# TensorE's order by an estimate of VectorE's backlog, and keys copied by ScalarE, in a fused attention and gated-MLP kernel

## The chip, the core and the metric

The kernel runs on one NeuronCore of a Trainium2 chip. Its engines are TensorE (PE in the profile, with its weight loads as PEld), VectorE (DVE), ScalarE (ACT), GpSimd (POOL) and SyncE (SP), which here only issues DMAs. Each engine executes its own instructions strictly in the order in which the program lists them; they wait for each other by semaphores. The metric is the device time of one execution in microseconds; the time of a kernel is the median of several runs.

## The reference

A sequence of 2048 tokens with 640 features is normalised per token. Branch A is attention with 32 heads of 20 features over 4 segments of 512 tokens, with a memory carried from segment to segment; branch B is a gated MLP with 1536 hidden features. All tensors are bf16.

```python
xn = _layernorm(x, axis=-1)
q, k, v = xn @ wq, xn @ wk, xn @ wv          # 32 heads x 20, 4 segments x 512
for s in range(4):
    p = softmax(qs @ ks.T * Dh**-0.5 + causal_mask)
    a_dot = p @ vs
    a_mem = (phi(qs) @ M) / (phi(qs) @ z + 1e-6)
    o = g * a_mem + (1.0 - g) * a_dot         # g = sigmoid(beta), per head
    M = M + phi(ks).T @ vs                    # phi(t) = t + 1 if t > 0 else exp(t)
    z = z + sum(phi(ks))
s = o @ wo
h = sigmoid(xn @ w_gate) * (xn @ w_up)
out = x + s * silu(h @ w_down)
```

## The kernel before

Four segments of 512 tokens are pipelined. While segment n has its attention scores computed, the same stretch of program also holds the projections of segment n+1, the MLP of segment n, and the output projection of segment n-1. A segment is cut into 20 slots (`NSLOT`). Each slot has one group of score matmuls (`Sps`, four row tiles side by side), one exponential of 2048 columns on ScalarE (`pt`), a causal select on GpSimd, and the weighing of an earlier group by the values (`Aps`, many matmuls of 21 columns). Between them the program puts matmul units from two sources:

- **tasks**, with a due time in slots. They are in a heap; when the position `pos` (in slots) passes a task's time, it is taken out. A task that is a generator (`k_chunk`, `q_chunk`, `q_bound`, `v_tile`, `o_proj`, `mem_read`, `m_update`) goes into the list `ready`; any other (a DMA, a step of VectorE) is issued at once. `later(lag, ...)` makes a task due `lag * R` slots from now, with R = 20/24.
- **bulk**, the gate, up and down projections of the MLP in their order.

`step` gives the next matmul: of the unit in hand, else of the first one in `ready`, else of bulk. `advance` moves `pos` by each matmul's cost (`T512` = 0.216 us for 512 columns, `T320` = 0.136) over the segment's budget for one slot. So the order on all engines is written out when the program is made; nothing is decided on the chip.

PSUM has 4 banks for the scores, one for `Aps` and three for everything else (the pool `ps_d`, tag "d"): a matmul unit needs one of these three, and it is free again when VectorE or ScalarE has read it. What each unit leaves to these engines:

- `k_chunk`: a copy of `psk` to bf16 (`evacuate`: ScalarE in segment 0, VectorE in the others), then a VectorE maximum of absolute values from the copy (`kabs`, L301). After chunks 2 and 4 the copy goes to DRAM (`stage_out`), and from there to `KT` in another layout (`relay`).
- `q_chunk`: the same copy (`q5`), then absolute values on VectorE (`aq`, L332). `q_bound` multiplies `aq` with `IK` (made from `kabs`) to a bound on each score (`cps`), which goes by `c_out` to DRAM (`Cs`) and by `c_in` into `QT`, where the score matmuls read it.
- `mem_read`: three VectorE instructions (L460 to L463) behind up to three short matmuls (`am`). `m_update`: two per chunk (L442, L443).
- gate: a tanh on ScalarE (`tg`). up: one VectorE instruction (`hT`, L492), which also reads `tg`. down: a tanh on ScalarE (`t`), then VectorE (`aa`, L509). `o_proj`: VectorE L557, and for the second half L563 and the store.
- phi (L400, L401, ScalarE L404, then L408): 5 chunks of k and 5 of q in a segment, at most two at a time.
- `weigh`: L607, L608, L610 on VectorE once per head group.

The startup is written by hand: weight loads and the first four blocks of x on SP's queue, warm-up matmuls, statistics (`ln_stats`), normalising (`ln_norm`, with a TensorE transpose `pT` in segment 0), values of segment 0 (`v_tile`), keys, queries, the staging of both through DRAM, and six units of bulk, before the first scores.

Of the kernel before, what the change touches and what calls it, by code (L numbers as in the profile page):

```python
# [10 lines left out]
P = 128  # L11
S = 2048
D = 640
# [3 lines left out]
NSEG = 4  # L17
# [38 lines left out]
T320 = 0.136  # L56
TPV = 0.0255


@with_exitstack  # L60
def kernel(
# [49 lines left out]
    def run(unit):  # L111
        for _ in unit:
            pass

    def step(keep):
        if cur[0] is None:
            if ready:
                cur[0] = ready.pop(0)
            elif len(bulk) > keep:
                _, fn, a = bulk.pop(0)  # L120
                cur[0] = fn(*a)
            else:
                return None
        cost = next(cur[0], None)
        if cost is None:
            cur[0] = None
            return 0.0
        return cost

    def advance(target, budget, keep):  # L130
        while True:
            while tasks and tasks[0][0] <= pos[0]:
                _, _, _, fn, a = heapq.heappop(tasks)
                if inspect.isgeneratorfunction(fn):
                    ready.append(fn(*a))
                else:
                    fn(*a)
            if pos[0] >= target:
                return
            cost = step(keep)  # L140
            if cost is None:
                pos[0] = min(target, tasks[0][0]) if tasks else target
            else:
                pos[0] += cost / budget
# [4 lines left out]
    def x_load(n, p):  # L149
        t = lnp.tile([P, 2, D], BF, name="xt2")  # L150
        st[n][f"x{p}"] = t
        r0 = n * L + 2 * p * P
        if n == 0:
            for i in range(2):
                nc.sync.dma_start(t[:, i, :], x2[r0 + i * P:r0 + (i + 1) * P, :])
        else:
            nc.sync.dma_start(t[:], x2[r0:r0 + 2 * P, :].rearrange("(i p) d -> p i d", p=P))

# [6 lines left out]

    x_load(0, 0)
    load_proj("v", A_wv, 0, HB)
    x_load(0, 1)
    load_proj("v", A_wv, HB, D)
# [10 lines left out]

    for i in range(2):
        load_glu(i, 0)
        load_glu(i, 1)

# [57 lines left out]
    def ln_stats(n, p, i0=0, i1=2):  # L242
        s = st[n]
        x = s[f"x{p}"]
        if i0 == 0:
            s[f"mv{p}"] = lnp.tile([P, 2, 2], F32, name="mv")
            s[f"rstd{p}"] = lnp.tile([P, 2], F32, name="rstd")
        mv, rstd = s[f"mv{p}"], s[f"rstd{p}"]
        for i in range(i0, i1):
            bs = lnp.tile([P, 2, 6], F32, name="bs")  # L250
            nc.vector.bn_stats(bs[:, 0, :], x[:, i, 0:HB])
            nc.vector.bn_stats(bs[:, 1, :], x[:, i, HB:D])
            nc.vector.bn_aggr(mv[:, i, :], bs[:])
        nc.gpsimd.tensor_scalar(rstd[:, i0:i1], mv[:, i0:i1, 1], EPS, None, op0=ALU.add)
        nc.gpsimd.tensor_tensor(rstd[:, i0:i1], rstd[:, i0:i1], nhalf[:, i0:i1], op=ALU.pow)

    def ln_norm(n, p, i):
        s = st[n]
        if "xnT" not in s:
            s["xnT"] = xpool.tile([P, DC, L], BF, name="xnT")  # L260
        xn = lnp.tile([P, D], BF, name="xn")
        nc.vector.tensor_scalar(xn[:], s[f"x{p}"][:, i, :], s[f"mv{p}"][:, i, 0:1], s[f"rstd{p}"][:, i:i + 1],
# [19 lines left out]

    def evacuate(n, dst, ps):
        if n == 0:
            nc.scalar.copy(dst, ps)
        else:
            nc.vector.tensor_copy(dst, ps)  # L287

    def k_chunk(n, c):
# [5 lines left out]
        for k in range(DC):  # L295
            nc.tensor.matmul(ps[:], lhsT=W["k"][:, k, c * P:(c + 1) * P], rhs=s["xnT"][:, k, :],  # L296
                             start=(k == 0), stop=(k == DC - 1))
            if k < DC - 1:
                yield T512
        evacuate(n, s["k5"][:, c, :], ps[:])  # L300
        nc.vector.tensor_reduce(out=s["kabs"][:, c:c + 1], in_=s["k5"][:, c, :], axis=AX.X, op=ALU.max,  # L301
                                apply_absolute_value=True)
        if c in (2, 4) and n:
            later(0.9, stage_out, n, c // 4, Ks, KT, "k5")
# [6 lines left out]
    def stage_out(n, half, src, dst, name):  # L311
        a, b = ((0, 3), (3, 5))[half]
        st[n][f"out_{name}"] = b
        nc.sync.dma_start(src[n % 2][a * P:b * P, :].rearrange("(c p) n -> p c n", p=P), st[n][name][:, a:b, :])
        if n:
            later(1.0, relay, n, half, src, dst)
            for c in range(a, b):
                later(1.9 if name == "q5" else 0.7, phi_push, n, name, c)

    def q_chunk(n, c):  # L320
# [5 lines left out]
        for k in range(DC):  # L326
            nc.tensor.matmul(ps[:], lhsT=W["q"][:, k, c * P:(c + 1) * P], rhs=s["xnT"][:, k, :],  # L327
                             start=(k == 0), stop=(k == DC - 1))
            if k < DC - 1:
                yield T512  # L330
        evacuate(n, s["q5"][:, c, :], ps[:])
        nc.vector.tensor_scalar(s["aq"][:, c, :].bitcast(U16), s["q5"][:, c, :].bitcast(U16), 0x7FFF, None,  # L332
                                op0=ALU.bitwise_and)
        if c in (2, 4) and n:
            later(0.9, stage_out, n, c // 4, Qs, QT, "q5")
        yield T512

# [58 lines left out]
    def phi(n, src, c):  # L396
# [4 lines left out]
        nc.vector.tensor_scalar(t, t, 1.0, None, op0=ALU.add)  # L401

        def exp():
            nc.scalar.activation(mn[:], mn[:], ACT.Exp)  # L404
            later(0.5, rest)

        def rest():
            nc.vector.tensor_tensor(t, t, mn[:], op=ALU.max)  # L408
            st[n][f"phi_{src}"] = c + 1
# [13 lines left out]
    def m_update(n, cs):  # L423
# [3 lines left out]
        for i, c in enumerate(cs):  # L427
            w = (H1[c] - H0[c]) * VW
            for j in range(4):
                nc.tensor.matmul(dm[:, i, 0:w], lhsT=s["pkt"][:, j, c * P:(c + 1) * P],  # L430
                                 rhs=V[4 * (n % 2) + j][:, H0[c]:H1[c], :].rearrange("p h e -> p (h e)"),
                                 start=(j == 0), stop=(j == 3))
            yield 4 * w / 2400
        for i, c in enumerate(cs):
            w = (H1[c] - H0[c]) * VW
# [9 lines left out]
    def mem_read(n, j, b):  # L445
# [7 lines left out]
        for i, c in enumerate(parts):  # L453
# [3 lines left out]
                             rhs=Mbd[:, c, lo - H0[c]:hi - H0[c], :].rearrange("p h e -> p (h e)"),  # L457
                             start=(i == 0), stop=True, skip_group_check=True)
        rm = opool.tile([P, 16], F32, name="rm", bufs=3)
        nc.vector.scalar_tensor_tensor(out=rm[:], in0=am[:, :, DH], scalar=1e-6,  # L460
# [21 lines left out]
    def up(n, f):  # L482
# [3 lines left out]
        for k in range(DC):  # L486
            nc.tensor.matmul(ps[:], lhsT=Wu[f // 4][:, k, fo:fo + P], rhs=s["xnT"][:, k, :],  # L487
                             start=(k == 0), stop=(k == DC - 1))
            if k < DC - 1:
                yield T512  # L490
        h = gpool.tile([P, L], BF, name="hT", bufs=FC)
        nc.vector.scalar_tensor_tensor(out=h[:], in0=s["tg"][:], scalar=1.0, in1=ps[:], op0=ALU.add, op1=ALU.mult)  # L492
# [3 lines left out]
    def down(n, j, half):  # L496
# [5 lines left out]
        for f in range(FC):  # L502
            nc.tensor.matmul(yp[:], lhsT=s["hT"][f][:, j * P:(j + 1) * P], rhs=W["d"][:, f, hs],  # L503
                             start=(f == 0), stop=(f == FC - 1))
            if f < FC - 1:
# [3 lines left out]
        nc.vector.scalar_tensor_tensor(out=s[f"aa{j}"][:, hs], in0=t2[:], scalar=1.0, in1=yp[:],  # L509
                                       op0=ALU.add, op1=ALU.mult)  # L510
        s[f"down{j}"] = half + 1
        yield T320


    def o_add(n, j, c0, c1):
        o = st[n]["od"][:, j, c0:c1]
        if n >= 1:
            nc.vector.tensor_tensor(o, o, st[n]["om"][:, j, c0:c1], op=ALU.add)
# [26 lines left out]
    def o_proj(n, j, half):  # L545
# [16 lines left out]
        elif half == 1:  # L562
            (nc.gpsimd if n == NSEG - 1 else nc.vector).tensor_tensor(xr, aa[:], xr, op=ALU.add)  # L563
            later(0.9, lambda: nc.sync.dma_start(o2[rows, :], xr))
        yield T320
# [22 lines left out]
    def weigh(n, pair, u, dg, pt):  # L588
# [10 lines left out]
        for (kb, off, qb) in blocks:  # L599
            for r in range(4):  # L600
# [3 lines left out]
                first = False  # L604
        if (u, dg) in ((2, 0), (4, 1)):
            rd = opool.tile([P, 4, 4], F32, name="rd", bufs=3)
            nc.vector.reciprocal(rd[:], A[:, :, :, DH])  # L607
# [19 lines left out]
    def startup():  # L627
# [4 lines left out]
        ln_norm(0, 0, 0)  # L632
        warm(10)
        ln_norm(0, 0, 1)
        ln_stats(0, 1, 0, 1)
        run(v_tile(0, 0, 0))
        ln_stats(0, 1, 1, 2)
        ln_norm(0, 1, 0)
        run(v_tile(0, 1, 0))
        ln_norm(0, 1, 1)  # L640
        run(v_tile(0, 2, 0))
        for j in range(3):
            run(v_tile(0, j, 1))
        v_ones(0, 4)
# [19 lines left out]
        stage_out(0, 1, Qs, QT, "q5")  # L664
        c_in(0, (0,))
        x_load(1, 0)
        x_load(1, 1)
# [14 lines left out]
    for n in range(NSEG):  # L682
        w = NSLOT * n
        m = n + 1
        if m < NSEG:
# [7 lines left out]
            for c in range(DC):  # L693
                at(w + R * (9.6 + 0.75 * c), 1.08, k_chunk, m, c)
                at(w + R * (13.4 + 0.75 * c), 1.08, q_chunk, m, c)
            at(w + R * (17.2), 1.12, q_bound, m)
            if m + 1 < NSEG:
# [5 lines left out]
            for i, cs in enumerate(([0, 1, 2], [3, 4])):  # L703
                at(w + R * (10.0 + i), 0.7, m_update, n, cs)
        if n >= 1:
            for j in range(4):
                at(w + R * (1.1 + 0.3 * j), 0.0, o_ready, n - 1, j)
                at(w + R * (4.0 + 0.5 * j if j < 3 else 9.6), 0.0, xr_load, n - 1, j)
            for i in range(8):
                at(w + R * (6.6 + i), 0.68, o_proj, n - 1, i // 2, i % 2)  # L710
                at(w + R * (4.0 + 0.75 * i), 0.2, mem_read, n, i // 2, i % 2)

# [8 lines left out]
    for n in range(NSEG):  # L721
# [6 lines left out]
        total += sum(t[2] for t in tasks if t[0] < NSLOT * (n + 1))  # L728
        total += 320 * TPV
        budget = total / NSLOT  # L730
        for slot in range(NSLOT):
            pair, u = divmod(slot, NU)
            now = NSLOT * n + slot
            pt = scores(n, pair, u)
            advance(now + 0.5, budget, keep)
            for w in due:
                weigh(*w)
                pos[0] += weigh_cost(w[2], w[3]) / budget
            due, held = held, []
# [60 lines left out]
```

## Time and profile before

| | us |
|---|---|
| median of 3 runs | 355.54 (354.80 to 355.67) |
| the profiled execution | 354.9 |
| its span | 353.2 |
| first key chunk (`psk`) starts | 14.03 |
| first scores of segments 0 to 3 start | 34.95, 106.5, 191.9, 271.6 |
| busy: VectorE, ScalarE | 231.4, 230.5 |

An excerpt of the costliest groups. Each line has line, engine, operation, output and inputs with shapes and the count; then busy time and mean ns of one; then the idle time of the engine just before these instructions and what ended it.

```profile
L581 ACT ACTIVATE pt<-Sps 128x2048 bf16<-128x2048 f32 x80 | 150.1, 1876 | 63.5 <-PE Sps L576 59.0
L492 DVE SCALAR_TENSOR_TENSOR hT<-tg,up 128x512 bf16<-128x512 bf16 x48 | 32.7, 680 | 36.1 <-PE up L487 27.5
L509 DVE SCALAR_TENSOR_TENSOR aa<-t,yp 128x320 bf16<-128x320 bf16 x32 | 15.5, 484 | 27.1 <-ACT t L508 27.0
```

Busy time of TensorE covers the pipeline of a matmul, and a waiting engine's idle time is given to what ended last before it went on. A chain of waits is read from the timeline: start, duration, engine, line, operation, tiles, and in brackets the idle time before it and its releaser.

### The profile page before, as it was taken

Reading aid. Unit: us, or ns where it says so; the run is one execution under the profiler, and the core shown is the slowest. Engines: PE = TensorE matmul, PEld = TensorE weight load, DVE = VectorE, ACT = ScalarE, POOL = GpSimd, SP = SyncE. Lnnn points to the kernel's source line nnn. Section 1 sums busy time; section 2 is a strip of 40 time slices with the busy share of each in tenths; the row PEclk is TensorE's granted clock in tenths of the full one; section 3 lists DMA queues with packets and bytes.
Section 4 is the critical chain, followed back from the end, with each engine's and each line's share of the span. In section 5 each row is a group of like instructions: output and inputs, shape, how many; then the busy total and the mean of one; then the engine's idle time right before and its main releaser. Section 6 shows DMA issues by size and latency. Waiting matters only on the chain.

```text
span 353.2 us, 8387 instructions
## 1 busy us (share of the span) xinstructions
PE 334.6 (95%) x3402; PEld 186.6 (53%) x3402; DVE 231.4 (66%) x581; ACT 230.5 (65%) x248; POOL 101.2 (29%) x135
## 2 busy tenths in 40 slices
PE   7899998999899989999999999999899999999995
PEld 6543444545564455644466455554346645544673
DVE  5342675489666666799856876699874577643365
ACT  3553877858797656546788656655688765778730
POOL 5930342232224322222222432223132322232214
PEclk9999999999999999999999999999999999999998
DMA  7964846557813521044930370114640421220042
GB/s 226 330 214 125 217 125 129 193 169 183 158 44 39 111 58 38 20 132 77 231 58 2 74 132 2 40 63 143 152 80 3 61 74 37 60 74 2 0 61 74
DMA packets 56581, 35.40 MB, mean 100 GB/s; under 512 B 31200, under 2 KB 56544, under 8 KB 56544
## 3 DMA queue, kind: packets, MB, share of 16 engines
q1 hardware_dynamic: 53024, 30.79, 35.8%
q10 hardware_dynamic: 3520, 4.10, 4.0%
q8 instruction: 26, 0.43, 0.5%
q14 instruction: 11, 0.09, 0.1%
HBM read 19.80 MB, written 8.00 MB: 79 GB/s over the span
## 4 chain that ended last, share of the span: by engine, by line
PE 67%; DVE 18%; issue 5%; DMA 5%; ACT 3%; POOL 1%; SPq 1%; ACTq 0%; DVEq 0%
PE yp L503 14%; PE up L487 13%; PE gp L474 12%; PE Aps L601 7%; PE Sps L576 6%; PE psv L369 4%; PE sp L553 4%; PE psk L296 3%; PE psq L327 3%; DVE aa L557 2%; DVE k L287 2%; DVE kabs L301 2%; DMA Ks<-k 2%; ACT pt L581 1%; DVE xr L563 1%
## 5 line engine op out<-in xcount | busy, mean ns | idle before, releaser
L581 ACT ACTIVATE pt<-Sps 128x2048 bf16<-128x2048 f32 x80 | 150.1, 1876 | 63.5 <-PE Sps L576 59.0
L584 POOL TENSOR_SCALAR_AFFINE_SELECT pt<-pt 128x1024 bf16<-128x1024 bf16 (+1 forms) x80 | 75.4, 943 | 230.6 <-ACT pt L581 230.6
L474 PE MATMUL gp<-xnT,Wg 128*128 128x512 bf16 x240 | 64.4, 379 | 2.8 <-DVE om L463 1.4
L487 PE MATMUL up<-xnT,Wu 128*128 128x512 bf16 x240 | 64.8, 379 | 0.7 <-DVE om L463 0.7
L503 PE MATMUL yp<-Wd,hT 128*128 128x320 bf16 x384 | 58.8, 299 | 0.0
L492 DVE SCALAR_TENSOR_TENSOR hT<-tg,up 128x512 bf16<-128x512 bf16 x48 | 32.7, 680 | 36.1 <-PE up L487 27.5
L601 PEld LDWEIGHTS <-pt 128*128 128x128 bf16 x1280 | 43.7, 96 | 16.0 <-issue 1.9
L601 PE MATMUL Aps<-va,pt 128*128 128x21 bf16 x1280 | 44.4, 172 | 0.2 <-DVE od L610 0.2
L503 PEld LDWEIGHTS <-hT 128*128 128x128 bf16 x384 | 34.7, 97 | 17.2 <-issue 4.6
L479 ACT ACTIVATE tg<-gp 128x512 bf16<-128x512 f32 x48 | 28.5, 595 | 14.3 <-PE gp L474 13.9
L474 PEld LDWEIGHTS <-Wg 128*128 128x128 bf16 x240 | 21.2, 97 | 26.3 <-issue 6.4
L487 PEld LDWEIGHTS <-Wu 128*128 128x128 bf16 x240 | 21.1, 97 | 24.1 <-issue 4.4
L509 DVE SCALAR_TENSOR_TENSOR aa<-t,yp 128x320 bf16<-128x320 bf16 x32 | 15.5, 484 | 27.1 <-ACT t L508 27.0
L576 PE MATMUL Sps<-QT,KT 21*128 21x128 bf16 (+3 forms) x512 | 31.7, 301 | 1.2 <-DMA QT<-Cs 0.8
L369 PE MATMUL psv<-Wv,xnT 128*128 128x320 bf16 x160 | 27.4, 299 | 1.5 <-DVE hT L492 0.7
L553 PE MATMUL sp<-Wo,oT 128*128 128x320 bf16 x160 | 27.1, 299 | 1.1 <-DVE rm L460 0.6
L327 PE MATMUL psq<-xnT,Wq 128*128 128x512 bf16 x100 | 24.9, 379 | 1.3 <-DVE aa L557 1.3
L296 PE MATMUL psk<-xnT,Wk 128*128 128x512 bf16 x100 | 25.0, 379 | 0.1
L404 ACT ACTIVATE mn<-mn 128x512 bf16<-128x512 bf16 x35 | 21.8, 628 | 4.5 <-DVE mn L400 4.5
L576 PEld LDWEIGHTS <-KT 21*128 21x128 bf16 x512 | 9.1, 92 | 27.8 <-issue 27.3
L557 DVE SCALAR_TENSOR_TENSOR aa<-aa,sp 128x320 bf16<-128x320 bf16 x32 | 15.5, 483 | 7.0 <-PE sp L553 6.8
L553 PEld LDWEIGHTS <-oT 128*128 128x128 bf16 x160 | 14.5, 97 | 9.6 <-issue 2.9
(74 smaller groups left out, 330.4 us busy)
## 6 DMA issues: line engine op xcount, KB each, us to landing
KT<-Ks SPq DMA_DIRECT2D x32, 80.0 KB
QT<-Qs SPq DMA_DIRECT2D x32, 80.0 KB
xr<-in_A_x_dram SPq DMA_DIRECT2D x15, 160.0 KB
out_dram<-xr SPq DMA_DIRECT2D x15, 160.0 KB
xt<-in_A_x_dram SPq DMA_DIRECT2D x6, 320.0 KB
Wd<-in_B_w_down_dram ACTq DMA_DIRECT2D x1, 1920.0 KB
Ks<-k SPq DMA_DIRECT2D x4, 384.0 KB
Qs<-q SPq DMA_DIRECT2D x4, 384.0 KB
```

Source lines behind the costliest of these rows:

```text
L296: nc.tensor.matmul(ps[:], lhsT=W["k"][:, k, c * P:(c + 1) * P], rhs=s["xnT"][:, k, :], start=(k == 0), stop=(k == DC - 1))
L327: nc.tensor.matmul(ps[:], lhsT=W["q"][:, k, c * P:(c + 1) * P], rhs=s["xnT"][:, k, :], start=(k == 0), stop=(k == DC - 1))
L369: nc.tensor.matmul(ps[:], lhsT=s["xnT"][:, k, j * P:(j + 1) * P], rhs=W["v"][:, k, half * HB:(half + 1) * HB], start=(k == 0), stop=(k == ...
L474: nc.tensor.matmul(gp[:], lhsT=Wg[f // 4][:, k, fo:fo + P], rhs=s["xnT"][:, k, :], start=(k == 0), stop=(k == DC - 1))
L487: nc.tensor.matmul(ps[:], lhsT=Wu[f // 4][:, k, fo:fo + P], rhs=s["xnT"][:, k, :], start=(k == 0), stop=(k == DC - 1))
L492: nc.vector.scalar_tensor_tensor(out=h[:], in0=s["tg"][:], scalar=1.0, in1=ps[:], op0=ALU.add, op1=ALU.mult)
L503: nc.tensor.matmul(yp[:], lhsT=s["hT"][f][:, j * P:(j + 1) * P], rhs=W["d"][:, f, hs], start=(f == 0), stop=(f == FC - 1))
L553: nc.tensor.matmul(sp[:], lhsT=s["oT"][:, j, c, :], rhs=W["o"][:, c, hs], start=(c == 0), stop=(c == DC - 1))
L576: nc.tensor.matmul(Sps[:, r, c0:c0 + ncol], lhsT=kt[32 * r:32 * r + VW, gi, kb * P:(kb + 1) * P], rhs=qt[32 * r:32 * r + VW, gi, kb * P:L] ...
L581: nc.scalar.activation(pt[:], Sps[:], ACT.Exp, scale=SCALE)
L584: nc.gpsimd.affine_select(out=diag, in_=diag, compare_op=ALU.is_ge, fill=0.0, base=0, pattern=[[0, 4], [0, cnt], [1, P]], channel_multipli ...
L601: nc.tensor.matmul(A[:, qb, r, :], lhsT=pt[:, r, off:off + P], rhs=V[4 * (n % 2) + kb][:, 4 * g + r, :], start=first, stop=True, skip_grou ...
```

## The change

Five things are changed.

1. The scheduler keeps two running sums while it writes the program: `work["PE"]`, the matmul time issued so far, and `work["DVE"]`, which each VectorE step raises by a fixed cost (`dve(cost)`), never below `work["PE"]`. Their difference is the estimate of VectorE's backlog, `behind()`. A ready unit is taken before bulk only if the backlog is under `AHEAD` = 1.0 us, if bulk is used up, or if the unit is more than `LATE` = 2 slots past its time.
2. Keys are copied by ScalarE in every segment, and the maximum of their absolute values is taken from PSUM, not from the copy.
3. Due times: memory reads come from 2.5 R on, each 1.1 R, instead of from 4.0 R, each 0.75 R; key and query chunks each 0.85 R instead of 0.75 R, queries from 13.8 R; `q_bound` 0.7 R after the last query chunk instead of at 17.2 R; `m_update` from 11.0 R, not 10.0 R; `o_proj` from 7.0 R, not 6.6 R; query phis 1.2 R after the staging, not 1.9 R; the loads of x for the residual from 6.5 R, and the last of them 0.6 R after the first store.
4. In the startup three blocks of x are loaded ahead of the first half of Wv (before: two), the statistics of block 2 come ahead of the normalising of block 1, and the value tiles are reordered.
5. The second part of Wu is loaded after the first `c_in`, not with the other weights.

```diff
+TSC = 0.5
+AHEAD = 1.0
+LATE = 2.0
...
+    work = {"PE": 0.0, "DVE": 0.0}
+
+    def dve(cost):
+        work["DVE"] = max(work["DVE"], work["PE"]) + cost
+
+    def behind():
+        return work["DVE"] - work["PE"]
+
     def step(keep):
         if cur[0] is None:
-            if ready:
-                cur[0] = ready.pop(0)
+            if ready and (len(bulk) <= keep or behind() < AHEAD or pos[0] - ready[0][0] > LATE):
+                cur[0] = ready.pop(0)[1]
             elif len(bulk) > keep:
...
+        work["PE"] += cost
         return cost
...
-    x_load(0, 0)
+    for j in range(3):
+        x_first(j)
     load_proj("v", A_wv, 0, HB)
-    x_load(0, 1)
+    x_first(3)
     load_proj("v", A_wv, HB, D)
...
-    for i in range(2):
-        load_glu(i, 0)
-        load_glu(i, 1)
+    load_glu(0, 0)
+    load_glu(0, 1)
+    load_glu(1, 0)
...
-        evacuate(n, s["k5"][:, c, :], ps[:])
-        nc.vector.tensor_reduce(out=s["kabs"][:, c:c + 1], in_=s["k5"][:, c, :], axis=AX.X, op=ALU.max,
+        nc.scalar.copy(s["k5"][:, c, :], ps[:])
+        nc.vector.tensor_reduce(out=s["kabs"][:, c:c + 1], in_=ps[:], axis=AX.X, op=ALU.max,
                                 apply_absolute_value=True)
+        dve(0.69)
...
+        if c == DC - 1 and n:
+            later(0.7, q_bound, n)
...
-            later(0.9, lambda: nc.sync.dma_start(o2[rows, :], xr))
+            def store():
+                nc.sync.dma_start(o2[rows, :], xr)
+                if j == 0 and n < NSEG - 1:
+                    later(0.6, xr_load, n, 3)
+            later(0.9, store)
...
         warm(10)
+        ln_stats(0, 1, 0, 1)
         ln_norm(0, 0, 1)
-        ln_stats(0, 1, 0, 1)
         run(v_tile(0, 0, 0))
         ln_stats(0, 1, 1, 2)
+        run(v_tile(0, 1, 0))
         ln_norm(0, 1, 0)
-        run(v_tile(0, 1, 0))
+        run(v_tile(0, 0, 1))
         ln_norm(0, 1, 1)
         run(v_tile(0, 2, 0))
-        for j in range(3):
-            run(v_tile(0, j, 1))
+        run(v_tile(0, 1, 1))
+        run(v_tile(0, 2, 1))
...
         c_in(0, (0,))
+        load_glu(1, 1)
         x_load(1, 0)
...
-                at(w + R * (9.6 + 0.75 * c), 1.08, k_chunk, m, c)
-                at(w + R * (13.4 + 0.75 * c), 1.08, q_chunk, m, c)
-            at(w + R * (17.2), 1.12, q_bound, m)
+                at(w + R * (9.6 + 0.85 * c), 1.08, k_chunk, m, c)
+                at(w + R * (13.8 + 0.85 * c), 1.08, q_chunk, m, c)
...
-                at(w + R * (6.6 + i), 0.68, o_proj, n - 1, i // 2, i % 2)
-                at(w + R * (4.0 + 0.75 * i), 0.2, mem_read, n, i // 2, i % 2)
+                at(w + R * (7.0 + 1.0 * i), 0.68, o_proj, n - 1, i // 2, i % 2)
+                at(w + R * (2.5 + 1.1 * i), 0.2, mem_read, n, i // 2, i % 2)
```

## The prediction

> **What bounds the kernel now.** I read the page first, then who TensorE (PE) waits for, then the engines by stretches of 9 us, then single stalls in the timeline.
>
> ```profile
> span 353.2 us, 8387 instructions
> PE 334.6 (95%) x3402; PEld 186.6 (53%) x3402; DVE 231.4 (66%) x581; ACT 230.5 (65%) x248; POOL 101.2 (29%) x135
> ```
>
> PE is the bound, but 95% overstates it: a matmul's record covers its pipeline too (379 ns for 512 columns). Its pace is the distance of starts, read from the timeline: 25 matmuls of `psk` span 5.56 us, their last record is 0.38, so one starts each 0.216 us (24 distances in 5.18). In the same way 320 columns take 0.136 us and a 21-column one 0.025. The counts of the groups times these paces give 308.2 us of pure work. The 80 score groups lose a further 20.1 us around them (about 0.2 each, when the array changes to four row tiles, and 4 of waiting), 1.4 us pass before the first matmul and 4.6 after the last start. 353.2 - 308.2 - 20.1 - 6.0 leaves **18.9 us of gaps**: 4.6 before the first key chunk, 14 in the four segments. I went through the starts that came late, with what released them. With the late score groups the main loop's gaps from the first scores on come to 14.7 us: **10.9 released by VectorE** (2.7, 3.1, 3.7 and 1.4 in segments 0 to 3) **and 3.8 by ScalarE**. One more, 1.0 us, is the wait of the first scores for a DMA.
>
> Who PE waits for, the first rows (us, times, longest):
>
> ```profile
> PE gp L474 <- DVE om L463: 1.4, 2, 1.0
> PE pT L269 <- DVE xn L262: 1.3, 1, 1.3
> PE psq L327 <- DVE aa L557: 1.3, 2, 0.8
> PE cps L342 <- DVE aq L332: 1.1, 1, 1.1
> PE cps L342 <- DVE hT L492: 0.9, 1, 0.9
> PE Sps L576 <- DMA QT<-Cs: 0.8, 1, 0.8
> ```
>
> Nearly all name VectorE (DVE): a PSUM tile of the three in `ps_d` that it hasn't emptied, or `aq`. Stretches (us; busy of PE, PEld, DVE, ACT, POOL):
>
> ```profile
> 144.00:153.00 9.00, 9.00 (x114) 5.93 (x115) 8.62 (x23) 4.67 (x5) 1.92 (x3) 1.00 0.06 21
> 153.00:162.00 9.00, 8.17 (x81) 4.00 (x78) 8.65 (x20) 3.96 (x3) 1.77 (x3) 1.00 0.41 131
> ...
> 234.00:243.00 9.00, 8.56 (x98) 4.48 (x94) 8.65 (x20) 4.36 (x4) 2.65 (x3) 1.00 0.41 129
> 243.00:252.00 9.00, 7.83 (x72) 3.40 (x71) 8.65 (x22) 5.57 (x6) 2.13 (x3) 1.00 0.43 124
> ```
>
> In the key and query stretches DVE is full (8.65 of 9) while over the span it is at 66%, and ACT has half its time free there. The clock is 1.00 throughout.
>
> **The change, part by part.**
>
> *Keys to ScalarE.* The rows (count | busy, mean ns):
>
> ```profile
> L287 DVE CAST k<-psk 128x512 bf16<-128x512 f32 x15 | 10.3, 684 | 0.9 <-PE psk L296 0.8
> L301 DVE TENSOR_REDUCE kabs<-k 128x1 f32<-128x512 bf16 x20 | 13.7, 686 | 7.1 <-ACT k L285 6.5
> L285 ACT CAST k<-psk 128x512 bf16<-128x512 f32 x5 | 2.9, 585 | 2.6 <-PE psk L296 2.6
> ```
>
> DVE loses 15 x 0.684 = 10.3 us, all in its full stretches; ACT gains 15 x 0.585 = 8.8. The maximum now reads PSUM, which no row shows: the lower bound is 0.680 (`hT`, 512 wide from PSUM), the upper 0.483 x 512/320 = 0.77 (`aa`, L557, from PSUM). The CAST above, which reads just this tile, is nearest: I take 0.69, no change; the upper end is 20 x 0.08 = 1.7 us of DVE, off the path but for a small part. The new cost is a wait: a key tile is now free after ScalarE and VectorE, and ScalarE may sit in an exponential of 1.88 us, one per slot of some 4 us: a chance of 0.47 of a mean 0.94, so 0.44 + 0.585 = 1.0 us before the copy is out. In segment 0 the copy is already followed by the maximum (15.31 + 0.58, then 15.93). Behind the maximum in DVE's queue stand `hT`, `aa`, `od`, and PE waits for those. Two more PSUM tiles are two units of 1.08 us of cover; ScalarE's own evacuations in the trace cost PE 1.36 us over 24 `va` units (0.06 each). Bounds for the 15: 0, and 15 x (1.88 + 0.585 - 2.16) = 15 x 0.3 = 4.5, if each copy meets a whole exponential; I take **+1.0**, a little over 15 x 0.06, since the tile now waits for two engines.
>
> [...]
>
> *The order by backlog, reads and queries spread.* No instruction is added. A ready unit (k, q, v, `o_proj`, `mem_read`, `m_update`) waits while VectorE's estimated backlog is 1.0 us or more and bulk (gate, up, down) is there, for 2 slots at most. A `mem_read` is 0.2 us of PE and 0.17 + 0.25 + 0.49 = 0.9 of DVE; eight come each 0.75 R = 0.625 slot before, each 1.1 R = 0.92 slot now. The gaps behind `am` (1.26, 0.17, 0.56, 0.81, 0.63 and some) are 3.8 us; I expect 3.0 back. `q_bound` is made ready 0.7 R = 0.58 slot after the last query chunk instead of at a fixed time; its waits are 1.44, 1.08 and 0.30 us. One of them:
>
> ```profile
> 248.78 0.29 DVE L332 TENSOR_SCALAR aq<-q 128x512 uint16<-128x512 uint16 x1
> 250.22 0.68 DVE L492 SCALAR_TENSOR_TENSOR hT<-tg,up 128x512 bf16<-128x512 bf16 x1
> 250.95 0.38 PE L342 MATMUL cps<-aq,IK 128*32 128x512 bf16 x1 [0.92 <-DVE hT L492]
> ```
>
> `cps` had to wait for `hT` because its PSUM tile was not empty. All 2.8 should go. The rest (`sp`, `psq`, `gp` behind DVE in the key and query stretches, 4.3 us) is what 10.3 us less DVE and the new order address: 1.8 back. Together **-7.6**, of 10.9; bounds 0 (the stalls only move) and -10.9, and -14.7 if ScalarE's went too.
>
> *Queues.* `xr_load` of j=3 comes after a store instead of at 9.6 R: SP's waits for that buffer (L543, 7.0 us in 5 times) shrink; the relays behind them are needed slots later: 0. Query phi 0.7 R earlier: same 1.0 us of DVE each, 0.
>
> *Startup.* Three row blocks come ahead of Wv and the statistics of block 2 ahead of xn of block 1.
>
> ```profile
> 8.91 0.45 DVE L262 TENSOR_SCALAR xn<-xt,mv,rstd 128x640 bf16<-128x640 bf16 x1
> 9.42 0.45 PE L269 MATMUL pT<-ident,xn 128*128 128x128 bf16 x5 [1.29 <-DVE xn L262]
> 14.03 5.56 PE L296 MATMUL psk<-xnT,Wk 128*128 128x512 bf16 x25
> 18.08 2.52 SPq L314 DMA_DIRECT2D Ks<-k  x2
> 34.95 0.40 PE L576 MATMUL Sps<-QT,KT 21*128 21x512 bf16 x4 [0.84 <-DMA QT<-Cs]
> 36.44 0.50 DVE L251 BATCH_NORM_STATS2 bs<-xt 128x6 f32<-128x320 bf16 x1 [1.53 <-DMA xt<-in_A_x_dram]
> ```
>
> Replayed with the rows' durations: xn0 5.25, statistics of block 2 to 6.75 (1.04 us), xn1 to 7.2, block 3 to 8.2, xn2 to 8.65, xn3 9.15 (after POOL's 0.9). PE: pT1 7.25, v(0,0) 7.6, v(1,0) to 9.15, pT2, v(0,1), pT3 10.2, three more of 0.68: keys start at 12.65, **1.35 earlier** than 14.03. Wu of i=1 (655 KB) no longer stands in the queue ahead of Ks, which took 5.4 us to land (18.08 to 23.5) where Qs, on a freer queue, took 3.2. Then KT's relays no longer hold SP until 25.0 and Qs goes out at its copy's end, so the chain Qs 3.2, relay 1.45, Cs 2.9, QT 2.2 ends about 32.0, and PE, through with its six units at 33.73 - 1.35 = 32.4, finds it landed: first scores at about 32.6, **-2.3**. What is late next: Wu moved ahead of x of segment 1 adds 655 KB / 330 GB/s (the page's busiest slice) = 2.0 us to a load that VectorE already waited 1.53 us for: issued from about 30.45 on, landed 3.0 + 2.0 later, 35.4, with VectorE free at 34.9 - 2.3 = 32.6. It stands 1.3 us longer; two free PSUM tiles cover most: **+0.2**, 1.3 if they do not.
>
> *Sum.* -7.6 + 1.0 - 2.3 + 0.2 = **-8.7**. The profiled execution took 354.9 (span 353.2 and 1.7 around): 346.2. The median of the runs, 355.54, lies 0.6 above it, so **346.8**.
>
> **Rivals.**
> - *ScalarE takes VectorE's place*: the key copies cost the 4.5 bound and ScalarE's stalls make half of the DVE gain vanish: -3.8 + 4.5 - 2.1 = -1.4, 354.1. For it: 3.8 us of ScalarE stalls already; against: ACT at 4 to 5.6 of 9 in just these stretches.
> - *The estimate is blind*: it knows no waits for ScalarE (27.0 us of DVE waiting for `t`), so backlog is underrated and the order stays nearly as it was. Left: startup, `q_bound`'s 2.8 and the keys, less 1.0: 355.5 - 2.1 - 2.8 - 1.8 + 1.0 = 349.8.
> - *Slower: the postponed queries make the next segment's scores late.* After `q_bound` come 0.67 slot to the store of Cs, 0.83 to its reading, and 2.2 us = 0.55 slot to land: it decides from slot 20 - 2.05 = 17.95. The last query chunk is due at 14.33; two postponements of 2 slots and 0.58 make 18.9: 0.95 slot x 4.0 us x 3 segments = 11.4, so 346.8 + 11.4 = 358.2. Against it: it takes the full postponement twice, and bulk runs out towards a segment's end, which lifts the rule.
>
> **Numbers.** Forecast 0.65 (341.5 to 351, its own range), blind estimate 0.11, ScalarE 0.11, late scores 0.13. 0.3% is 1.1 us, about what a measurement here can tell from none: faster 0.82 (forecast, blind and half of the ScalarE case), same 0.05, slower 0.13. Range 341.5 to 356: below it an all-gaps-gone case (0.06), above it most of the late scores.
>
> **What would show it.** Right: DVE busy near 221, ACT near 239; first `psk` near 12.7 and first scores near 32.6; `cps` no longer waits; DVE below 8 of 9 in the key stretches; PE's gaps released by DVE near 3 us. Wrong: PE waits for ACT `k` of several us, `kabs` waiting long for it; `Sps` waiting for QT<-Cs at the segments' starts; gaps as large as before behind other tiles.

## The result, and the profile after

The changed kernel takes 358.37 us (median of 6 runs, 356.87 to 360.98); the kernel before took 355.03 beside it (6 runs). The ratio is 1.0101, with a 95% interval of 1.0055 to 1.0147: **about 1% slower**, where 346.8 had been forecast. The profiled execution took 358.6, its span is 356.8. One execution is left out of the medians below, 354.99 us of the run "All but the rule", which lay 1.6% above the fastest of its kernel.

The head of the page of the changed kernel:

```profile
span 356.8 us, 8337 instructions
PE 332.1 (93%) x3359; PEld 185.8 (52%) x3402; DVE 222.8 (62%) x566; ACT 237.7 (67%) x263; POOL 101.6 (28%) x135
```

VectorE has 8.6 us less to do and ScalarE 7.2 more, close to what was forecast (221 and 239). TensorE's work is the same; 43 of its 3402 records are missing in this trace. So the loss must be waiting, or matmuls that run slower. Who TensorE waited for, the first rows (us, times, longest):

```profile
PE Sps L608 <- DMA QT<-Cs: 3.7, 1, 3.7
PE yp L526 <- DMA Wd<-in_B_w_down_dram: 2.7, 1, 2.7
PE wps L658 <- POOL ident L209: 1.4, 1, 1.4
PE pT L285 <- DVE xn L278: 1.0, 2, 0.7
PE Aps L633 <- DVE od L643: 1.0, 2, 0.8
PE psk L306 <- DVE kabs L311: 1.0, 2, 0.5
```

Before, nearly every row named VectorE. The two largest are now DMAs: the scores of segment 1 wait 3.7 us for the bound `Cs`, and the first down unit waits 2.7 us for its weights. Before, TensorE waited for `Cs` only at the very first scores, 0.8 us, and for Wd not at all. The small waits of `cps` have gone, as forecast.

The segments say where to look. First scores of segments 0 to 3 start at 32.5, 112.6, 197.2 and 276.8 us (before: 34.95, 106.5, 191.9, 271.6). Segment 0 takes 80.1 us instead of 71.6; segments 1, 2 and the rest take 84.6, 79.6 and 80.0 instead of 85.4, 79.7 and 81.6. **The whole loss is 8.5 us in segment 0**, against 2.4 won before it and 2.5 after it.

Stretches of the changed kernel around these two waits (us; busy PE, PEld, DVE, ACT, POOL; then granted clock, DMA share, GB/s):

```profile
60.00:63.00 3.00, 3.00 (x36) 1.70 (x34) 0.00 (x0) 2.62 (x5) 1.10 (x1) 1.00 1.07 370
63.00:66.00 3.00, 0.35 (x2) 0.00 (x0) 0.69 (x1) 1.37 (x1) 0.68 (x1) 0.92 0.83 262
66.00:69.00 3.00, 2.99 (x19) 1.82 (x20) 0.92 (x3) 0.00 (x0) 0.00 (x0) 0.51 0.00 0
69.00:72.00 3.00, 3.00 (x49) 2.03 (x48) 0.49 (x1) 2.30 (x3) 0.00 (x0) 1.00 0.00 0
108.90:112.50 3.60, 0.00 (x0) 0.00 (x0) 2.93 (x8) 1.05 (x3) 1.10 (x1) 1.00 0.05 13
112.50:116.30 3.80, 3.58 (x12) 1.40 (x14) 1.04 (x4) 2.88 (x3) 1.15 (x3) 0.61 0.00 0
116.30:120.00 3.70, 3.70 (x38) 1.77 (x37) 2.21 (x6) 1.70 (x2) 0.43 (x1) 0.94 0.22 43
```

Two things are to be seen. After the two waits the granted clock is 0.51 and 0.61 in the next stretch. Counted by the missing part of the clock, that is 3.0 x 0.49 = 1.5 us after the first, and 3.8 x 0.39 + 3.7 x 0.06 = 1.7 us after the second. With 2.7 and 3.7 us of waiting the two events cost an estimated 9.6 us in this execution. And between 60 and 63 us VectorE is idle, 0.00 of 3, while the scheduler had written out this stretch as one in which VectorE is far behind.

The key stretches, for comparison with those shown of before:

```profile
153.00:162.00 9.00, 8.89 (x100) 5.23 (x101) 5.52 (x17) 6.06 (x6) 1.84 (x2) 1.00 0.06 21
243.00:252.00 9.00, 8.30 (x85) 4.59 (x85) 6.00 (x14) 6.34 (x7) 2.40 (x2) 1.00 0.28 91
```

VectorE has come down from 8.65 to 5.5 and 6.0 of 9 in these two, but they are stretches of the same time and not of the same work. The key and query units of segment 1 ran from 142.7 to 167.9 us before; now they are spread over 149.5 to 183.3, and from 171 to 180 us VectorE is again at 8.62 of 9. So the forecast "below 8 of 9 in the key stretches" came true only in part, and segments 1 and 2 are hardly faster. The group of the maximum shows a likely reason:

```profile
L311 DVE TENSOR_REDUCE kabs<-psk 128x1 f32<-128x512 f32 x20 | 13.8, 690 | 28.6 <-ACT k L310 28.5
```

It costs the same from PSUM (690 ns, 686 from the copy), but VectorE stood 28.5 us in front of it waiting for ScalarE's copy; before, 6.5 us.

### The profile page after: what moved, and what is told of

Read it like the earlier page. It is cut to its first block, busy times and chain, and to the rows that moved or that the text cites. A ratio compares the mean times of both kernels' runs of the same rounds, so it can differ in the third digit from the quotient of the medians.

```text
span 356.8 us, 8337 instructions
## 1 busy us (share of the span) xinstructions
PE 332.1 (93%) x3359; PEld 185.8 (52%) x3402; DVE 222.8 (62%) x566; ACT 237.7 (67%) x263; POOL 101.6 (28%) x135
## 4 chain that ended last, share of the span: by engine, by line
PE 65%; DVE 16%; DMA 7%; issue 5%; ACT 5%; POOL 0%; ACTq 0%; SPq 0%; DVEq 0%
PE gp L496 11%; PE up L509 11%; PE yp L526 11%; PE Aps L633 6%; PE sp L578 5%; PE Sps L608 5%; PE psv L386 5%; PE psk L306 4%; PE psq L338 3%; DMA Wd<-in_B_w_down_dram 2%; ACT pt L613 2%; DMA xt<-in_A_x_dram 2%; DVE mn L417 2%; DVE q L345 1%; DVE hT L515 1%
## 5 line engine op out<-in xcount | busy, mean ns | idle before, releaser
L509 PE MATMUL up<-xnT,Wu 128*128 128x512 bf16 x228 | 63.6, 384 | 2.0 <-DVE hT L515 1.0
L496 PE MATMUL gp<-xnT,Wg 128*128 128x512 bf16 x223 | 61.7, 383 | 3.1 <-DVE hT L515 0.8
L526 PE MATMUL yp<-Wd,hT 128*128 128x320 bf16 x384 | 61.4, 304 | 2.7 <-DMA Wd<-in_B_w_down_dram 2.7
L515 DVE SCALAR_TENSOR_TENSOR hT<-tg,up 128x512 bf16<-128x512 bf16 x48 | 32.6, 679 | 28.3 <-PE up L509 26.1
L501 ACT ACTIVATE tg<-gp 128x512 bf16<-128x512 f32 x48 | 28.5, 594 | 21.3 <-PE gp L496 19.3
L311 DVE TENSOR_REDUCE kabs<-psk 128x1 f32<-128x512 f32 x20 | 13.8, 690 | 28.6 <-ACT k L310 28.5
L338 PE MATMUL psq<-xnT,Wq 128*128 128x512 bf16 x92 | 24.0, 379 | 0.6 <-issue 0.2
```

The source lines that it names most:

```text
L496: nc.tensor.matmul(gp[:], lhsT=Wg[f // 4][:, k, fo:fo + P], rhs=s["xnT"][:, k, :], start=(k == 0), stop=(k == DC - 1))
```

## The experiments

Each was timed beside the kernel before on its chip (354.1 to 354.5 us there). Theory W (waits): the rule that postpones units makes both waits of segment 0, each followed by slow matmuls. Rival K (keys): VectorE standing behind ScalarE's copies is the loss. Rival M: postponing only moves stalls about. Waits are given as the profile lists them, and the time of a segment is taken from the first scores of one to those of the next, in the profiled execution.

### Undoing one thing in the changed kernel

**The down weights earlier.**

```diff
-    at(6.8, 0, load_late, "d", B_w_down)
+    at(4.4, 0, load_late, "d", B_w_down)
```

> The load of Wd is issued 2.4 slots earlier (due 4.4, not 6.8); nothing else differs from the changed kernel. Theory W (two waits that postponing makes in segment 0, each followed by a stretch at half the matmul rate, are the loss): the 2.8 us wait of yp for Wd and the 1.3 us of slow matmuls behind it go, 358.4 to about 354.3; the wait of the scores for Cs (3.7) stays. Rival K (the keys on ScalarE make VectorE stand, 22 us in the main loop) and rival M (postponing only moves stalls about): the freed time is lost again to VectorE within the segment, 357 to 358.5.

353.95 us, 0.998 of before (0.9962 to 0.9998). The wait for Wd and the slow stretch behind it are gone (the granted clock is 1.00 from 63 to 69 us), and the 4.3 us (ratios 1.0101 and 0.998) were not lost again. Segment 0 takes 75.4 us. Theory W holds for this half; the wait for Cs stays, 3.1 us.

**No postponing in segment 0.**

```diff
-            if ready and (len(bulk) <= keep or behind() < AHEAD or pos[0] - ready[0][0] > LATE):
+            if ready and (len(bulk) <= keep or behind() < AHEAD or pos[0] - ready[0][0] > LATE or pos[0] < NSLOT):
```

> Ready units are never postponed in segment 0 (positions under 20 slots); segments 1 to 3 keep the rule. Theory W: keys and queries of segment 0 come back to their due times, Ks goes out near 73 us instead of 83, Cs lands before the scores of segment 1, and down units no longer come before Wd: both waits go with their slow stretches, 358.4 - 2.8 - 1.3 - 3.7 - 1.7 = about 349, with some 1 to 2 us of VectorE waits back: 349 to 351. Rival M: as many VectorE waits return in segment 0 as before the change (2.7 us) and more behind the keys; 354 or more. Rival K: 355 to 357, since ScalarE's copies stay.

351.15 us, 0.9902 (0.9879 to 0.9925). Both DMA waits of segment 0 are gone; it takes 73.7 us.

**No postponing at all.**

```diff
-            if ready and (len(bulk) <= keep or behind() < AHEAD or pos[0] - ready[0][0] > LATE):
+            if ready:
```

> Ready units always go first, in all segments (the order of before, with the new due times and the keys on ScalarE). Theory W: like the run without postponing in segment 0, but the rule's gain in segments 1 and 2 is lost; each of them has at most 3 us of it, so 350 to 354. Rival M: no worse than that run, 349 or below. Rival K: 355 or more, slower than before although no order is changed.

349.62 us, 0.9859 (0.9839 to 0.9879), a little below the run before it (segments 1 to 3: 84.1, 77.2, 80.3 against 83.1, 79.4, 80.0). Together these segments take 241.6 us without the rule and 242.5 with it, so it brings nothing there.

**Keys back on VectorE, rule kept** (copy by VectorE in segments 1 to 3, maximum from the copy, `dve(1.37)`).

> Keys of segments 1 to 3 are copied by VectorE again and the maximum is taken from the copy (backlog cost 1.37 instead of 0.69); the rest is the changed kernel. Theory W: the two waits stay, and VectorE has 10.3 us more to do in its full stretches, so more is postponed: 359 to 364. Rival K: VectorE no longer stands for ScalarE's copies; 350 to 355.

362.94 us, 1.0244 (1.0228 to 1.0259). With VectorE back at the copies the loss is larger, so rival K is out as its cause. The higher cost in the estimate changes the order as well, and more is postponed: the wait for Cs grows to 5.2 us before segment 1, three such waits add up to 7.1, and the one for Wd is 2.9.

### One part alone, put into the kernel before

With all three parts and the rule taken out, the order on every engine is that of the kernel before, so the four runs divide the change.

**The startup alone** (x order, value tiles, place of Wu).

> The kernel before with the new startup alone (three blocks of x ahead of Wv, value tiles reordered, the second part of Wu after c_in). Theory W: keys start near 12.5 and first scores near 32.5 instead of 34.9, less about 0.5 to 1 us because VectorE then waits longer for x of segment 1: 352 to 353.5 where before is 354.3. Rival: later work is bound elsewhere and hides it, 354 or more.

353.92 us, 0.998 (0.9965 to 0.9995). The first scores start at 32.8, 2.1 earlier, and most of it is given back 3 to 7 us later: segment 0 takes 72.9 us instead of 71.6. VectorE in this run, start, duration, and idle time before in brackets:

```profile
32.68 0.69 DVE L513 SCALAR_TENSOR_TENSOR hT<-tg,up 128x512 bf16<-128x512 bf16 x1 [1.47 <-PE up L507]
36.50 0.49 DVE L266 BATCH_NORM_STATS2 bs<-xt 128x6 f32<-128x320 bf16 x1 [3.13 <-DMA xt<-in_A_x_dram]
...
38.54 0.64 DVE L513 SCALAR_TENSOR_TENSOR hT<-tg,up 128x512 bf16<-128x512 bf16 x1
```

x of segment 1 now stands behind Wu, the statistics wait 3.13 us for it (1.53 before, 2.50 in the changed kernel), and `hT` waits behind them in VectorE's queue. TensorE then waits 1.1 us for that `hT`.

**The rule alone** (keys on VectorE, old due times, old startup).

> The kernel before with the postponing rule alone (keys on VectorE, counted 1.37; old due times, q_bound at its fixed 17.2 R). Theory W: keys and queries of segment 0 are postponed, Ks goes out near 80 us or later, the scores of segment 1 wait for Cs, down waits for Wd, and slow matmuls follow: 357 to 364. Rival M: the stalls only move, 353 to 355.

363.97 us, 1.0246 (1.02 to 1.0293): 9.6 us slower, the largest effect of the four. The wait for Wd is there (2.6). With `q_bound` at its fixed due time the scores wait for no DMA at the segments' starts, but `cps` waits three times, 4.1 us in all (the longest 1.9 and 1.4), for `aq` of query chunks that the rule had put right in front of it. The wait for Wd and these two are each followed by 3.4 us at a granted clock of 0.50 (over the whole execution, span 362.7 us, its mean is 0.986). The expectation was wrong in that the scores would wait for Cs: this wait came only together with the new due times.

**The keys alone.**

> The kernel before with the keys on ScalarE and the maximum from PSUM alone (old order, old due times). Theory W: VectorE has 10.3 us less in its full stretches, some of its 10.4 us of gaps goes and ScalarE's grow a little: 351 to 353.5. Rival K: the maximum makes VectorE stand for ScalarE's copy behind an exponential, as much as it saves: 354 to 357.

354.30 us, 1.0004 (0.9984 to 1.0025): nothing. Its group and one place in its timeline:

```profile
L313 DVE TENSOR_REDUCE kabs<-psk 128x1 f32<-128x512 f32 x20 | 13.6, 688 | 17.0 <-ACT k L312 17.0
```

```profile
150.94 1.88 ACT L611 ACTIVATE pt<-Sps 128x2048 bf16<-128x2048 f32 x1 [2.05 <-PE Sps L606]
152.71 0.58 ACT L312 CAST k<-psk 128x512 bf16<-128x512 f32 x1
...
153.32 0.69 DVE L313 TENSOR_REDUCE kabs<-psk 128x1 f32<-128x512 f32 x1 [2.33 <-ACT k L312]
153.53 0.59 ACT L312 CAST k<-psk 128x512 bf16<-128x512 f32 x1 [0.25 <-PE psk L308]
153.93 0.48 DVE L582 SCALAR_TENSOR_TENSOR aa<-aa,sp 128x320 bf16<-128x320 bf16 x1
```

The copy waits for an exponential, and VectorE stands 2.33 us at the maximum, with `aa` behind it. Over the kernel it stands there 17.0 us instead of 6.5, 10.5 more. That alone proves little: when 10.3 us of work are taken off an engine and the time stays, its idle time must grow by as much somewhere. TensorE's waits say more. Those for VectorE (over 0.2 us each, from the first scores on) add up to **7.4 us before and 7.4 here**. The 1.3 us of `psq` for `aa` have gone, and these have come or grown (`cps` for `aq` was 1.1):

```profile
PE cps L359 <- DVE aq L349: 1.7, 2, 1.1
PE psk L308 <- DVE kabs L313: 0.6, 1, 0.6
PE psq L340 <- DVE kabs L313: 0.5, 1, 0.5
```

So rival K's price is real, but it cancels a gain; it does not make the loss.

**The due times alone** (memory reads, keys and queries, `q_bound`, `o_proj`, `m_update`, residual loads).

> The kernel before with the new due times alone (memory reads spread, queries later, q_bound after the last query chunk, o_proj and m_update later). Theory W: the waits behind am and cps (6.6 us in the kernel before) go in part, but the queries come later by 0.4 R and more; 352 to 354.5. Rival: the later chain alone, with no rule, already makes the scores of segment 1 wait: 355 or more, and then it was not the rule.

348.73 us, 0.9839 (0.9818 to 0.9861): 5.6 us faster, below the expectation, and most of what the best runs below reach (6.2 to 7.1). TensorE's waits for VectorE, added up as above, fall from 7.4 to 3.0 us: those of `cps` are gone, and those for `om` of the memory reads fall from 2.1 us to 0.6. Its key stretches:

```profile
153.00:162.00 9.00, 8.67 (x81) 4.27 (x80) 8.69 (x20) 5.35 (x6) 2.20 (x2) 1.00 0.31 99
243.00:252.00 9.00, 8.88 (x83) 3.87 (x81) 8.66 (x22) 6.62 (x8) 2.25 (x3) 1.00 0.42 107
```

VectorE is as full as before (8.69 and 8.66 of 9), and TensorE stands less. So a full VectorE does not by itself make the gaps. That bursts of its work made them, which the new due times spread, fits the two kinds of waits that went; which of the due times did how much was not tried.

The four parts add up to -0.4 + 9.6 + 0.0 - 5.6 = +3.6, and the change measured +3.3. That they agree so closely is in part chance: the rule makes other waits alone than in the changed kernel, where it costs 8.6 us (ratios 1.0101 and 0.9859), and the other three together gave -5.0, not -6.0.

### What is left of the parts when the others are right

Four runs with x of segment 1 moved ahead of Wu.

**All but the rule.**

> The changed kernel without postponing, and x of segment 1 loaded ahead of the second part of Wu. If the startup's gain of 2.3 us at the first scores is given back because VectorE stands for x behind Wu (2.5 us, then hT late and TensorE waiting 1.0 to 1.4 for it), the gap of about 1 us near 38 us goes: 349.6 to about 348.5. If Wu is only late in its turn, up of chunk 4 waits for it and nothing is won: 349.6.

349.41 us (of 349.28, 349.41 and 352.70), 0.9885 (0.9828 to 0.9942). It is the second alternative: the gap behind x went, up of chunk 4 now waits 2.8 us for Wu, and nothing is won. The four runs share this wait, with 2.2 to 3.4 us:

```profile
PE up L509 <- DMA Wu<-in_B_w_up_dram: 2.9, 1, 2.9
```

(the waits of the run with due times and startup).

**The rule for units outside the chain of keys, queries and values only.**

> The same with the postponing rule back, but not for keys, queries, q_bound and values, whose results other stages wait for. If the loss is the late chain and not postponing as such: no wait of the scores for Cs and none of down for Wd, 347.5 to 349.5, beside 348.5 without any rule. If postponing as such harms, 351 or more.

352.79 us, 0.9952 (0.9927 to 0.9977). By the total this is on the side of "harms as such", but TensorE waits 3.4 us for Wu here, the intervals of the two runs overlap, and segment by segment the profiled executions take nearly the same, 75.5, 83.9, 77.5, 80.1 here and 76.2, 84.1, 77.2, 80.3 us without a rule. Inconclusive because of Wu; it is repeated below without that wait.

**Due times and startup, keys on VectorE.**

> New due times and new startup with x ahead of Wu; keys on VectorE as before; no rule. Due times alone gave 348.7 and the startup 2.3 us at the first scores: 346.4 to 347.5. Against the run with keys on ScalarE (expected 348.5) it tells whether the keys on ScalarE cost 1 to 2 us once the order is good.

351.49 us, 0.9918 (0.9888 to 0.9948): a miss, by the same wait.

**The maximum half a slot later, from the copy in SBUF** (`later(0.5, k_max, n, c)` in place of the reduction).

> As the run before, with keys copied by ScalarE and the maximum taken from the copy in SBUF, half a slot later, so that VectorE need not stand for ScalarE at the head of its queue, and the PSUM tile is free after the copy. If VectorE's standing (11 us more idle before kabs) is what ate the 10.3 us saved: kabs waits for ScalarE 6 us or less in all, and 345 to 346.5. If the keys bring nothing for another reason: as the run with keys on VectorE.

351.03 us, 0.9902 (0.9875 to 0.9929). `kabs` still waits 10.1 us for ScalarE, where 6 or less was expected. Segment 2 falls from 77.7 to 76.1 us, but a wait of 2.4 us for Cs appears before segment 1, so nothing is left.

The second part of Wu was then put behind the first store of the queries, where the DMA engines still had gaps (in the run with due times and startup a share of 0.03 from 21 to 22 us and of 0.00 from 26 to 27):

```diff
             elif c == 2:
                 stage_out(0, 0, Qs, QT, "q5")
+                load_glu(1, 1)
...
         c_in(0, (0,))
-        load_glu(1, 1)
         x_load(1, 0)
```

**Due times and startup with Wu there.**

> New due times and new startup, keys on VectorE, no rule; the second part of Wu is issued right behind the first store of the queries (about 22 us), where the DMA engines had been idle. If the startup's gain was eaten only by the place of Wu: first scores near 32.5 to 33, no wait for x over 1 us, none for Wu; 348.7 - 2 = 346 to 347.5. If Wu there delays the query relay, first scores come at 34 or later and it is as with due times alone, 348.7.

347.51 us, 0.9824 (0.9791 to 0.9858). No wait for Wu; the first scores start at 33.5 after 1.0 us of waiting for Cs.

**The same with keys on ScalarE.**

> The same with keys on ScalarE and the maximum from PSUM at once: the changed kernel without the rule and with Wu in this place. If the keys' gain is eaten by VectorE standing behind ScalarE's copy: g1 plus 0 to 1.5 us, 346.5 to 349, kabs waiting 17 to 20 us for ScalarE. If the keys help once nothing else is wrong: 1 to 2 us below g1.

349.48 us, 0.9873 (0.9824 to 0.9922): 2 us above, in segment 0 and its start (1.8 us of waiting for Cs; 72.3 against 70.7 us); `kabs` waits 19.5 us for ScalarE. The intervals of the two ratios overlap, so the keys are shown to bring nothing, and only likely to cost.

**Keys on ScalarE, maximum later, queries and Cs earlier.**

> g1 with keys on ScalarE, the maximum half a slot later from the copy in SBUF, queries due from 13.4 R, and the store of Cs 0.3 R after q_bound instead of 0.8 R, so that it stands ahead of the second query relay on SP. kabs no longer waits; 1 to 2 us below g1, 344.5 to 346.5. If the keys are worthless in any form: as g1.

347.95 us, 0.9841 (0.9785 to 0.9898). The expected 1 to 2 us did not come: `kabs` still waits 10.1 us in all, and TensorE now waits for query copies on VectorE (0.8 and 0.7 us). Whether a better place for the maximum would win something stays open.

**The rule outside the chain, with Wu in its good place.**

> g2 with the postponing rule, but not for keys, queries, q_bound and values. If the rule harms only by delaying the chain: within 1 us of g2. If postponing memory reads, output projection and memory updates harms in itself: 2 us or more above g2.

349.48 us, 0.986 (0.9837 to 0.9884), the same as without a rule. Postponing memory reads, `o_proj` and `m_update` shows neither harm nor good; so the harm of the rule comes from postponing the units that others wait for.

### Why segment 0

The scheduler's own numbers, written down while the program of the changed kernel was made (position in slots, estimated backlog, ready units, the first of them and how late it is):

```
0.00  behind 11.45 nready 0 head None
4.87  behind 10.81 nready 2 head v_tile  late 0.53
6.08  behind  8.76 nready 4 head v_tile  late 1.75
7.03  behind  6.11 nready 3 head v_tile  late 1.87
9.84  behind -1.10 nready 5 head k_chunk late 1.84
16.86 behind  0.81 nready 1 head q_chunk late 2.52
17.90 behind  0.42 nready 1 head q_bound late 0.17
```

The startup runs its units with `run`, which does not go through `step`, where TensorE's time is added; their VectorE costs are added all the same: four blocks at 1.15 and 0.45, five keys at 0.69, three `hT` at 0.7 make 11.95, less 0.5 for the first scores: 11.45. So segment 0 begins with a backlog that does not exist. Up to slot 9 the ready units wait about two slots each: first the value tiles, which ScalarE empties, then the keys behind them in the same list. Bulk is eaten meanwhile, and down comes at slot 8, at 63 us, before Wd has landed at 66.0. (The weights had been asked for at 57.4 us.)

**The estimate set to zero after the startup.**

```diff
     startup()
+    work["DVE"] = work["PE"]
     at(1.8, 0, load_glu, 2, 0)
```

> The changed kernel with the estimated backlog set to zero at the end of the startup; nothing else. With it, as the program is written out, down units begin near slot 10.7 instead of 8.1, but the last query chunk still goes at slot 16.9 and q_bound at 17.9. If the startup's sum makes the Wd wait alone: that wait and its slow matmuls go, the scores of segment 1 still wait 3 to 4 us for Cs, about 354 (as with Wd loaded early). If it makes both: 350 to 351.5.

353.46 us, 0.9959 (0.9937 to 0.9981), as expected of the first alternative: the wait for Wd has gone, the one for Cs is there with 3.1 us. So the false sum makes the one wait, and the rule itself, with an estimate that starts at zero, makes the other.

**Wu right before the reading of Cs, no rule, keys on VectorE.**

> New due times and new startup, keys on VectorE, no rule; the second part of Wu issued right before the first reading of Cs, near 27.7 us, while SP otherwise waits for Cs to land. If place alone was wrong: first scores near 32.6 to 33, x of segment 1 no later than with due times alone less the shift, no wait for Wu; 346 to 347.5. If Wu then delays the reading of Cs: first scores 34 or later, 348 or more.

347.66 us, 0.9801 (0.9777 to 0.9825), the same as the run with Wu behind the query store. These two are the fastest; **both beat both kernels**, by 1.8 to 2.0% against the one before.

## Why the prediction was wrong, step by step

- **The startup** was right to 0.2 us as far as it was replayed (keys at 12.50 where 12.65 was forecast, first scores at 32.51 where it was 32.6). The price of Wu ahead of x was mis-sized: +0.2 was taken, 1.3 was the bound, and segment 0 took 1.3 us longer in the run with the startup alone. The part is worth 0.4 us there (0.2 to 1.2 by its interval), not 2.1.
- **The keys**: the gain was counted in TensorE's gaps, and the price as the holding of a PSUM tile (+1.0). That ScalarE's copy comes late was worked out, 1.0 us each; that VectorE stands for that time *at the head of its queue* was written down but not priced. The +1.0 leaned on segment 0, where copy and maximum follow each other with TensorE at full pace (25 matmuls of `psk` in 5.56 us before); but there ScalarE has no exponentials yet, the first (`pt`) starts at 35.5 us. What came instead is 10.5 us of standing for 10.3 us of work saved, and the same 7.4 us of waits of TensorE; the part is worth 0.0 us.
- **Reads and queries** (3.0 + 2.8 = 5.8 forecast): the due times alone gave 5.6. The mechanism held, as the waits of `cps` and for `om` show; that the size fits so well is in part luck, since other due times were changed in the same run.
- **The rule** is the step that failed. In the sum it was taken for a reordering that can only give TensorE something better to do (it shares in the last 1.8 of the 7.6 us), whose bound was that the stalls only move; that it makes new waits was priced at nothing there and left to a rival. In truth it costs 9.6 us alone and 8.6 in the changed kernel, there chiefly by the waits for Wd (2.7) and Cs (3.7) and the slower matmuls behind them (an estimated 1.5 and 1.7). Two things were in reach and not followed up: which units it can hold back, among them value tiles that VectorE never touches; and what the estimate holds when segment 0 begins, since `run` passes by `step`. The rival "the estimate is blind" had the sign wrong: it was too high, not too low. What is late when bulk comes sooner, the load of Wd, was not asked at all.
- **The slower rival** named the right place, the scores waiting for QT<-Cs. It was given 0.13 and three segments; it came at one, for 3.7 us. The length of its chain was right: 2.05 slots of 4.0 us are 8.2, and from the end of `q_bound` (104.3 us) to the scores (112.56) it is 8.3. But the point from which it decides, slot 17.95, holds for the end of `q_bound` and not for its turn. Its turn came at slot 17.9 in the scheduler's count; its matmuls were done at 104.3 us, only 4.6 us ahead of the time when TensorE was ready for the scores (112.56 - 3.67 = 108.9). Of the 8.3 us, 1.1 are the bound's copy waiting for an exponential on ScalarE, and 1.2 its store waiting behind the second query relay on SP.

The chain in the changed kernel, the copy on ScalarE and SP's own issues:

```profile
103.48 0.82 PE L359 MATMUL cps<-aq,IK 128*32 128x512 bf16 x3
103.66 1.88 ACT L613 ACTIVATE pt<-Sps 128x2048 bf16<-128x2048 f32 x1 [0.19 <-PE Sps L608]
105.43 0.56 ACT L364 CAST cb<-cps 32x512 bf16<-32x512 f32 x1
105.65 1.43 SPq L297 DMA_DIRECT2D QT<-Qs  x4
107.18 0.32 SPq L373 DMA_DIRECT2D Cs<-cb  x1
110.24 1.12 SPq L380 DMA_DIRECT2D QT<-Cs  x2
```

- **The clock** was taken as 1.00 throughout. That the waits of 2.7 and 3.7 us for a DMA were followed by stretches at 0.51 and 0.61, an estimated 1.5 and 1.7 us more, was in no term.

## What to carry to other kernels

An estimate that orders work must be zero when the machine is idle and must count only what the unit in question needs: log it beside the program and hold it against the trace, where an engine that is "6 us behind" shows 0.00 busy. Before units are postponed, follow each one's result to the next wait, and ask also what comes *sooner* in their place and whether its data is there. And taking work off an engine gained nothing here, where the engine then stood, in its queue, for the one that took it.

## What the runs showed of the hardware

TensorE at half rate beside idle stretches of 1.4 to 3.7 us was not expected. In the changed kernel the granted clock is 0.50 from 65.53 to 68.94 us and from 113.32 to 116.73, 3.41 us each time. The waits of 2.7 and 3.7 us end at 66.01 and 112.56, so the first of these stretches begins 0.5 us before TensorE goes on, the second 0.8 us after it. In the second, four matmuls of 512 columns (`up`, from 114.61 us) take 1.70 us up to the start of the next matmul, 0.43 each, where one started each 0.216 us in the kernel before. The length of the wait alone does not decide it. In the kernel with the maximum half a slot later a wait of 2.2 us was not followed by it, and one of 2.4 us was (they end at 38.6 and 108.6 us):

```profile
38.60:42.00 3.40, 3.38 (x36) 1.63 (x37) 1.90 (x5) 0.84 (x3) 0.93 (x1) 1.00 0.95 230
...
108.60:112.00 3.40, 3.07 (x11) 1.13 (x13) 1.43 (x5) 2.47 (x2) 0.85 (x2) 0.52 0.00 0
```

In the run with the rule alone, waits of 1.9 and 1.4 us were followed by a clock of 0.50 over 3.4 us; in the run with the rule outside the chain and Wu late, a wait of 3.4 us was followed by one of 1.00 (40.8 to 44.2 us; the mean over that execution is 0.999). The same program differs from execution to execution, too: the six of the changed kernel have mean granted clocks of 0.985, 0.989, 0.989, 0.990, 0.994 and 0.997, and take 360.98, 360.12, 358.61, 358.12, 356.90 and 356.87 us. So the slower matmuls are part of the loss in most executions; the one with hardly any, 356.87 us, is still slower than the kernel before (353.97 to 355.67).
